# Channel attention followed by a gated convolution: decoding the filter taps earlier and moving the rounding copy of the gated product

## The chip, the cores and the metric

The kernel runs on one core of one Trainium2 chip. The metric is device time in microseconds (us) of one execution, from launch to the last write. Engines are named as in the profile: PE is TensorE (PEld its weight loads), DVE is VectorE, ACT is ScalarE, POOL is GpSimd, SP is SyncE, which here only issues transfers. A trailing q (SPq, ACTq) means the engine's instruction queue, where transfers are issued.

## The reference

```python
# q, k, v: (4, 6336, 256) float32; w_val, w_out: (256, 256); conv_w: (5, 256)
qn = q / (np.linalg.norm(q, axis=1, keepdims=True) + 1e-06)
kn = k / (np.linalg.norm(k, axis=1, keepdims=True) + 1e-06)
s = kn.transpose(0, 2, 1) @ qn / tau          # 256 x 256 scores per batch
a = softmax(s)                                 # over the last axis
x = v @ a                                      # (4, 6336, 256)
gate = sigmoid(sum over k of conv_w[k] * x shifted by k rows)   # 5 taps, causal
out = (gate * (x @ w_val)) @ w_out
```

The three small weight arrays arrive as 64-bit floating point numbers, everything else as float32. The attention is over channels: the scores of a batch are sums over its 6336 rows, so a batch's q and k have to be read to the end before its softmax, and only after that can its v be processed.

## The kernel before, in words

**Score groups.** The 6336 rows of q and k of a batch lie on 128 partitions with 49 rows each, and 64 rows remain. They are cut into 17 groups of three (the first and the fourth of two, the fourth with the remaining 64 rows). `load_group` (L78) issues the two transfers of a group on SP into one of six `raw` tiles, some groups ahead of use. `score_group` (L239) does three things with a group. It splits rows into a rounded part and a remainder (tile `hi`: an ACT cast at L269, a POOL subtraction at L270), for products in three fast passes. It squares the rows (L288, ACT, tile `sq`, three buffers) and adds the squares up for the norms (L293, on DVE for `acc_ps`, on POOL for `acc`). And it returns the matrix products (L316, PE, tile `s_ps`). In the first four groups of batches 0 and 1 no row is split, and the products are taken straight from `raw` in plain float32; in the other groups of batch 0 only the third row of a group, now and then none, is split.

**Weights.** As PE, ACT and POOL have no use for 64-bit numbers, DVE puts each weight together from its two words with integer operations: `decode` (L146 to L166) with ten operations for the taps (tiles `wk`, `wk_raw`, 10 partitions by 128, L204 and L206 the last two), `decode_past` for `w_val` (tiles `bits` and `wa`), and `decode` again for `w_out` (tile `wb`).

**Softmax.** `softmax` (L328) is a generator; each `tick()` emits one further stage at high priority. It makes `a`, its split form `w`, then turns `a` on PE (L395, into `at_ps`, one of four PSUM banks with the tag "bank"), copies it to `at` on ACT (L399) and multiplies it by `w_val` (L404), so that x @ w_val is one product of v as well.

**Steps.** The output is made in 13 chunks of 508 rows for each batch (52 steps). For a step, `transpose_v` (L436) turns v on PE (`t_ps`, tag "bank") and splits it on ACT and DVE; `conv` (L462) makes x in PSUM (`x_ps`, two buffers), takes the first tap on ACT (L469) and the other four on DVE (L471); `sigmoid` (L474) follows on ACT; `value` (L479) multiplies with x @ w_val; `split_g` (L491) rounds the product to `g_hi` on ACT (L502) and makes the remainder `g_lo` on POOL (L503); `finish` (L506) multiplies with w_out (`o_ps`, tag "bank"), copies the result to `o_sb` on ACT (L529) and stores it. In the main loop (L691) the steps of a batch run beside the score groups of the next batches, and beside its softmax.

**Order.** The order on each engine is made when the kernel is built, by a planner with simulated clocks: among the operations that it takes to be ready it issues the one that stands earliest in the program, with `high_priority` blocks ahead. Two things bind it: what an operation reads and writes, and `behind(...)` (L548), which puts an edge from a marked instruction to every later one of the same engine that is emitted within the block. It makes one engine's instruction stand behind another in its queue, and makes no engine wait for another. Tiles in one PSUM bank are given to one engine at a time.

Of the kernel before, what the change touches and what calls it, by code (L numbers as in the profile page):

```python
# [17 lines left out]
P = 128  # L18
# [6 lines left out]
EARLY = 2  # L25
# [6 lines left out]
def kernel(  # L32
# [45 lines left out]
    def load_group(b, g):  # L78
        j0, n = groups[g]
        t = raw_p.tile([P, 2, GROUP, C], F32, name="raw")  # L80
        for s, src in ((0, q), (1, k)):
            main = src[b, 0:RP * P].rearrange("(p j) c -> p j c", j=RP)
            last_load[0] = nc.sync.dma_start(out=t[:, s, 0:n, :], in_=main[:, j0:j0 + n, :])  # L83
            if rest_of(g):
                nc.sync.dma_start(out=t[0:REST, s, n, :], in_=src[b, RP * P:N])
        raws[b, g] = t

    for g in range(3):
# [150 lines left out]
    def score_group(b, g):  # L239


        n = groups[g][1]
        raw = raws.pop((b, g))
        rows_of = raw.rearrange("p s j c -> p j s c")
        if b == 0:
            if g < FIRST_SPLIT:
                nw, nv = GROUP, 2
            else:
                nw, nv = GROUP - 1, 2 + (g % 4 == 3)
        else:  # L250
            nw, nv = (GROUP, 2 * (g % 2 == 0)) if b == 1 and g < LEAD else (0, 2)
        parts = [(P, 0, n)]
        if rest_of(g):
            parts.append((REST, n, 1))
        if g == 0:
            state[b] = dict(
                s=ps_s.tile([P, NH, C], F32, name="s_ps"),
                acc=ps_s.tile([P, 2, C], F32, name="acc_ps"),
                side=acc_p.tile([P, 2, C], F32, name="acc"),
                begun=set(),  # L260
            )
        st = state[b]
        split = [(np_, max(j0, nw), j0 + nj) for np_, j0, nj in parts if j0 + nj > nw]
        hi = split_p.tile([P, GROUP, 2, 2, C], F32R, name="hi") if split else None
        sq = split_p.tile([P, GROUP, 2, C], F32, name="sq")
        cast = None
        for np_, ja, jb in split:
            r, js = slice(0, np_), slice(ja, jb)
            cast = nc.scalar.copy(hi[r, js, :, 0, :], rows_of[r, js])  # L269
            nc.gpsimd.tensor_tensor(hi[r, js, :, 1, :], rows_of[r, js], hi[r, js, :, 0, :].bitcast(F32), ALU.subtract)  # L270
        rows = [(np_, j) for np_, j0, nj in parts for j in range(j0, j0 + nj)]

        def norms():

            where = {}
            squares = [(np_, j0, j0 + nj) for np_, j0, nj in parts]
            for key in ("acc", "side"):
                if key not in st["begun"]:

                    full = [j for np_, j in rows if np_ == P and (j < nv) == (key == "acc")]  # L280
                    if full:
                        st["begun"].add(key)
                        where[full[0]] = key
                        nc.scalar.activation(st[key], rows_of[:, full[0]], AF.Square)
                        squares = [(np_, x, y) for np_, ja, jb in squares
                                   for x, y in ((ja, min(jb, full[0])), (max(ja, full[0] + 1), jb)) if x < y]
            for np_, ja, jb in squares:
                nc.scalar.activation(sq[0:np_, ja:jb], rows_of[0:np_, ja:jb], AF.Square)  # L288
            for np_, j in rows:
                if j in where:  # L290
                    continue
                eng, key = (nc.vector, "acc") if j < nv or np_ < P else (nc.gpsimd, "side")
                add = eng.tensor_tensor(st[key][0:np_], st[key][0:np_], sq[0:np_, j], ALU.add)  # L293
                if eng is nc.vector:
                    marks["ADD"] = add

        late = b == 1 and 0 < g < LEAD
        with tc.issue_after(cast.ins) if cast else nullcontext():
            if owed:
                owed.pop()()  # L300
            if b == 1 and LEAD <= g < LEAD + OWE:
                owed.append(norms)
            elif not late:
                norms()

        def mms(np_, j):
            r = slice(0, np_)
            stop = g == NG - 1 and np_ == parts[-1][0] and j == parts[-1][1] + parts[-1][2] - 1
            for h in range(NH):
                hs = slice(h * P, (h + 1) * P)  # L310
                if j < nw:
                    ops = [(raw[r, 1, j, hs], raw[r, 0, j, :])]
                else:
                    ops = [(hi[r, j, 1, x, hs], hi[r, j, 0, y, :]) for x, y in ((0, 0), (0, 1), (1, 0))]
                for n_, (lhs, rhs) in enumerate(ops):
                    marks["SCORES"] = nc.tensor.matmul(st["s"][:, h, :], lhs, rhs, start=False,  # L316
                                                       stop=stop and h == NH - 1 and n_ == len(ops) - 1)

        def clear():

            nc.tensor.matmul(st["s"].rearrange("p h c -> p (h c)"), zeros[:, 0:P], zeros, start=True, stop=False)

        if late:
            later.append(norms)
        return ([clear] if g == 0 else []) + [lambda np_=np_, j=j: mms(np_, j) for np_, j0, nj in parts for j in range(j0, j0 + nj)]


    def softmax(b):  # L328
# [63 lines left out]
        at_ps = ps.tile([P, 512], F32, name="o_ps", tag="bank")  # L392
        for h in range(NH):
            for h2 in range(NH):
                nc.tensor.transpose(at_ps[:, (h2 * NH + h) * P:(h2 * NH + h + 1) * P],  # L395
                                    a[:, h, h2 * P:(h2 + 1) * P], ident)
        yield
        at = soft_p.tile([P, NH, C], F32, name="at")
        note("ACT", nc.scalar.copy(at.rearrange("p h c -> p (h c)"), at_ps))  # L399
        yield  # L400
        aw_ps = ps.tile([P, 512], F32, name="o_ps", tag="bank")
        for h in range(NH):
# [59 lines left out]
    def conv(b, i, h):  # L462
        w = chunks[i][1]
        if h == 0:
            gates[b, i] = w_p.tile([P, NH, WMAX], F32, name="gate")
        gate = gates[b, i]
        x_ps = ps.tile([P, 512], F32, name="x_ps", bufs=2)
        product(x_ps[:, 0:HALO + w], weights[b], 0, b, i, h, 0, HALO + w)
        marks["TAP"] = nc.scalar.activation(gate[:, h, 0:w], x_ps[:, 0:w], AF.Copy, scale=cw[:, h:h + 1])  # L469
        for tap in range(1, K):  # L470
            marks["GATE"] = nc.vector.scalar_tensor_tensor(gate[:, h, 0:w], x_ps[:, tap:tap + w], cw[:, tap * NH + h:tap * NH + h + 1],  # L471
                                                           gate[:, h, 0:w], ALU.mult, ALU.add)
# [33 lines left out]
    def finish(b, i):  # L506
# [4 lines left out]
        o_sb = w_p.tile([P, NT, C], F32, name="o_sb")  # L511
        for j in range(0, nt, 2):
            pair = offs[j:j + 2]
            o_ps = ps.tile([P, 512], F32, name="o_ps", tag="bank")
            for u, off in enumerate(pair):
                n_ = 0
                for h in range(NH):
                    for gs, ws in ((gh, wo_hi), (gh, wo_lo), (gl, wo_hi)):
                        nc.tensor.matmul(o_ps[:, u * C:(u + 1) * C], gs[:, h, off:off + P], ws[:, h, :],  # L519
# [2 lines left out]
            if (b, i) == all_steps[-1]:  # L522

                for u, (copy, dma) in enumerate(((nc.scalar.copy, nc.scalar), (nc.vector.tensor_copy, nc.sync))[:len(pair)]):
                    copy(o_sb[:, j + u, :], o_ps[:, u * C:(u + 1) * C])
                    first = max((j + u) * P - pair[u], 0)
                    dma.dma_start(out=out[b, t0 + pair[u] + first:t0 + pair[u] + P], in_=o_sb[first:P, j + u, :])
                continue
# [60 lines left out]


    for n in range(NG):
        if n == 1:
            load_taps()
            load_weights(0)
            for _ in prepare_weights(2):
                pass
            prep.append(prepare_weights(0))
        if n == NG - 4:
            load_upto(NG + 1)
# [5 lines left out]
                load_v(*step(1))  # L605
        with behind(*(["SPIN"] if n < 2 else [])):
            run_group()
        if n == 0:
            with behind("SCORES"):
                spin(4)  # L610
        if n == 9:
            with behind("SCORES", "ADD"):
                spread_tau()
# [41 lines left out]
    tick()  # L655
    for h in range(NH):
        conv(*step(0), h)
    marks["TAP0"] = marks["TAP"]
    while stages:
        tick()  # L660
    for h in range(NH):
# [29 lines left out]
    for n in range(len(all_steps)):  # L691
# [1 line left out]
        if step(n + VLEAD + 1):  # L693
            load_v(*step(n + VLEAD + 1))
        turns = due_after(n) - (issued - len(ready))
        if n == 0:
            sigmoid(*now)
        for turn in range(turns):
            if turn == 0:
                run_group()  # L700
                with behind(*(["ACT", "VH", "SIG"] if n < EARLY else ["ACT"])):
                    split_group()
        tick()
        if n:
# [12 lines left out]
        with end(n + 1):  # L717
            value(*now)
        tick()
        with end(n + 1):  # L720
            split_g(*now)
        for turn in range(turns):
            if turn == 1:
                run_group()
                with behind(*(["TAP", "GH"] if n < EARLY else ["ACT"])):
                    split_group()
        if new:
            for h in range(NH):
                transpose_v(*new, h)
        tick()  # L730
        if prev:
            with behind(*{len(all_steps) - 2: ["CONV"], len(all_steps) - 1: ["G"]}.get(n, [])):
                finish(*prev)
# [33 lines left out]
```

## Time and profile before

| what | value |
|---|---|
| runs of the kernel before | 649.90, 649.97 and 649.16 us; median 649.9 |
| profiled execution, its own time | 649.27 us |
| span of the profile, first to last instruction | 647.4 us |
| PE busy | 635.9 us, 98% of the span |
| DVE, ACT, POOL busy | 523.4, 470.9 and 391.3 us |
| mean granted TensorE clock | 0.995 of full speed |

Times inside the span start at the span's first instruction. In a row of the timeline the first number is the start, the second the time taken, then come engine, line, operation, what is written from what, shape and count; a bracket at the end gives the idle time of the engine before the row and what ended it. In the view of waits a row has the total in us, the count and the longest.

### The profile page before, as it was taken

Reading aid. Unit: us, or ns where it says so; the run is one execution under the profiler, and the core shown is the slowest. Engines: PE = TensorE matmul, PEld = TensorE weight load, DVE = VectorE, ACT = ScalarE, POOL = GpSimd, SP = SyncE. Lnnn points to the kernel's source line nnn. Section 1 sums busy time; section 2 is a strip of 40 time slices with the busy share of each in tenths; the row PEclk is TensorE's granted clock in tenths of the full one; section 3 lists DMA queues with packets and bytes.
Section 4 is the critical chain, followed back from the end, with each engine's and each line's share of the span. In section 5 each row is a group of like instructions: output and inputs, shape, how many; then the busy total and the mean of one; then the engine's idle time right before and its main releaser. Section 6 shows DMA issues by size and latency. Waiting matters only on the chain.

```text
span 647.4 us, 10814 instructions
## 1 busy us (share of the span) xinstructions
PE 635.9 (98%) x4051; PEld 573.0 (89%) x4051; DVE 523.4 (81%) x826; ACT 470.9 (73%) x620; POOL 391.3 (60%) x205
## 2 busy tenths in 40 slices
PE   9999999999999999999999999999999999999996
PEld 7888889999888999999998989999998898888886
DVE  4999798787787878878787869777878889888884
ACT  5677797858787697778788688778679565655564
POOL 2784599768655598859765559686775222212221
PEclk9989999999999999999999999999999999999998
DMA  8989665455434556545543546552322343343213
GB/s 299 402 294 347 207 230 172 151 191 184 128 118 146 196 177 207 181 147 174 166 159 99 190 154 223 189 170 66 97 80 67 123 132 110 106 131 107 64 41 111
DMA packets 73674, 105.77 MB, mean 163 GB/s; under 512 B 4300, under 2 KB 55702, under 8 KB 73622
## 3 DMA queue, kind: packets, MB, share of 16 engines
q1 hardware_dynamic: 47846, 79.76, 37.0%
q10 hardware_dynamic: 25776, 25.32, 12.5%
q8 instruction: 32, 0.52, 0.3%
q14 instruction: 20, 0.16, 0.1%
HBM read 79.11 MB, written 25.95 MB: 162 GB/s over the span
## 4 chain that ended last, share of the span: by engine, by line
PE 86%; DVE 5%; ACT 3%; POOL 2%; issue 1%; DMA 1%; SPq 1%; ACTq 0%; POOLq 0%
PE o_ps L519 21%; PE x_ps L455 20%; PE s_ps L316 19%; PE val_ps L455 19%; PE t_ps L445 6%; DVE gate L471 2%; DMA raw<-in_k_dram 1%; POOL hi L270 1%; PE o_ps L404 1%; DVE acc_ps L293 1%; SPq L83 0%; ACT L477 0%; ACT L375 0%; ACT sq L288 0%; POOL g_lo L503 0%
## 5 line engine op out<-in xcount | busy, mean ns | idle before, releaser
L471 DVE SCALAR_TENSOR_TENSOR gate<-x_ps,cw,gate 128x508 f32<-128x508 f32 (+1 forms) x416 | 276.6, 720 | 12.6 <-ACT gate L469 10.6
L270 POOL TENSOR_TENSOR hi<-raw,hi 128x1536 fp32r<-128x1536 f32 (+3 forms) x62 | 180.3, 2911 | 81.7 <-ACT hi L269 81.7
L503 POOL TENSOR_TENSOR g_lo<-gate,g_hi 128x1016 fp32r<-128x1016 f32 (+1 forms) x50 | 116.2, 2324 | 110.2 <-ACT g_hi L502 101.1
L293 DVE TENSOR_TENSOR acc_ps<-acc_ps,sq 128x512 f32<-128x512 f32 (+1 forms) x135 | 94.1, 697 | 71.0 <-ACT sq L288 68.6
L455 PE MATMUL x_ps<-v_hi,w 128*128 128x512 f32 (+1 forms) x416 | 140.2, 394 | 0.9 <-DVE rz L379 0.9
L316 PE MATMUL s_ps<-hi 128*128 128x256 f32 (+1 forms) x912 | 131.6, 289 | 2.8 <-POOL hi L270 2.6
L455 PE MATMUL val_ps<-v_hi,w 128*128 128x508 f32 (+1 forms) x416 | 133.8, 383 | 0.0
L316 PEld LDWEIGHTS s_ps<-hi 128*128 128x128 f32 (+1 forms) x912 | 118.6, 191 | 7.7 <-POOL hi L270 3.6
L529 ACT COPY o_sb<-o_ps 128x512 f32<-128x512 f32 x99 | 58.2, 588 | 78.3 <-PE o_ps L519 78.1
L519 PE MATMUL o_ps<-wo_hi,g_hi 128*128 128x256 f32 x400 | 113.3, 283 | 1.3 <-ACT at L399 1.3
L519 PE MATMUL o_ps<-wo_hi,g_lo 128*128 128x256 f32 x400 | 112.3, 281 | 0.0
L519 PE MATMUL o_ps<-wo_lo,g_hi 128*128 128x256 f32 x400 | 112.2, 281 | 0.0
L288 ACT ACTIVATE sq<-raw 128x1536 f32<-128x1536 f32 (+2 forms) x72 | 96.0, 1342 | 4.9 <-DVE acc_ps L293 3.9
L455 PEld LDWEIGHTS x_ps<-v_hi,w 128*128 128x128 f32 x416 | 77.4, 188 | 15.3 <-ACT z L377 1.3
L455 PEld LDWEIGHTS val_ps<-v_hi,w 128*128 128x128 f32 x416 | 77.1, 188 | 13.6
L293 POOL TENSOR_TENSOR acc<-acc,sq 128x512 f32<-128x512 f32 x57 | 74.5, 1306 | 23.2 <-ACT sq L288 23.0
L469 ACT ACTIVATE gate<-x_ps,cw 128x508 f32<-128x508 f32 (+1 forms) x104 | 68.4, 670 | 20.8 <-PE x_ps L455 20.2
L269 ACT CAST hi<-raw 128x1536 fp32r<-128x1536 f32 (+3 forms) x62 | 76.8, 1241 | 5.7 <-PE s_ps L316 2.0
L446 ACT CAST v_hi<-t_ps 128x512 fp32r<-128x512 f32 (+1 forms) x104 | 56.1, 567 | 33.9 <-PE t_ps L445 31.3
L455 PE MATMUL x_ps<-v_lo,w 128*128 128x512 f32 (+1 forms) x208 | 79.6, 382 | 0.0
L455 PE MATMUL val_ps<-v_lo,w 128*128 128x508 f32 (+1 forms) x208 | 79.1, 380 | 0.0
L489 DVE TENSOR_TENSOR gate<-val_ps,gate 128x508 f32<-128x508 f32 (+1 forms) x104 | 64.1, 658 | 17.4 <-ACT gate L477 17.2
(114 smaller groups left out, 819.4 us busy)
## 6 DMA issues: line engine op xcount, KB each, us to landing
raw<-in_q_dram SPq DMA_DIRECT2D x60, 384.0 KB
raw<-in_k_dram SPq DMA_DIRECT2D x60, 384.0 KB
v_raw<-in_v_dram SPq DMA_DIRECT2D x44, 512.0 KB
out_dram<-o_sb ACTq DMA_DIRECT2D x47, 384.0 KB
out_dram<-o_sb ACTq DMA_DIRECT2D x47, 124.0 KB
raw<-in_q_dram SPq DMA_DIRECT2D x8, 256.0 KB
raw<-in_k_dram SPq DMA_DIRECT2D x8, 256.0 KB
v_raw<-in_v_dram SPq DMA_DIRECT2D x4, 384.0 KB
```

What stands on the lines that cost most here:

```text
L269: cast = nc.scalar.copy(hi[r, js, :, 0, :], rows_of[r, js])
L270: nc.gpsimd.tensor_tensor(hi[r, js, :, 1, :], rows_of[r, js], hi[r, js, :, 0, :].bitcast(F32), ALU.subtract)
L288: nc.scalar.activation(sq[0:np_, ja:jb], rows_of[0:np_, ja:jb], AF.Square)
L293: add = eng.tensor_tensor(st[key][0:np_], st[key][0:np_], sq[0:np_, j], ALU.add)
L316: marks["SCORES"] = nc.tensor.matmul(st["s"][:, h, :], lhs, rhs, start=False, stop=stop and h == NH - 1 and n_ == len(ops) - 1)
L455: marks["PRODUCT"] = nc.tensor.matmul(ps, wt[:, which, ws, ch, hs], vs[:, ch, lo:hi_], start=ws == 0 and ch == 0 and vs is th, stop=ws == ...
L469: marks["TAP"] = nc.scalar.activation(gate[:, h, 0:w], x_ps[:, 0:w], AF.Copy, scale=cw[:, h:h + 1])
L471: marks["GATE"] = nc.vector.scalar_tensor_tensor(gate[:, h, 0:w], x_ps[:, tap:tap + w], cw[:, tap * NH + h:tap * NH + h + 1], gate[:, h, 0 ...
L489: nc.vector.tensor_tensor(gate[:, h, 0:w], vals[h][:, 0:w], gate[:, h, 0:w], ALU.mult)
L503: nc.gpsimd.tensor_tensor(gl[:, :, 0:w], gate[:, :, 0:w], gh[:, :, 0:w].bitcast(F32), ALU.subtract)
L519: nc.tensor.matmul(o_ps[:, u * C:(u + 1) * C], gs[:, h, off:off + P], ws[:, h, :], start=n_ == 0, stop=n_ == 3 * NH - 1)
L529: marks["ACT"] = nc.scalar.copy(o_sb[:, j:j + len(pair), :], o_ps[:, 0:len(pair) * C].rearrange("p (j c) -> p j c", c=C))
```

## The change

Part by part:

1. The transfer of the second group of batch 0 is issued in two pieces for each of q and k: its first row of each partition, then the other two (`load_group`).
2. `load_taps()` and the ten decoding operations of the taps (`prepare_weights(2)`) come before the first group in the program, right behind the loads of groups 0 to 2, in place of before the second group. `load_weights(0)` stays where it was.
3. The four idle products on `warm` (`spin(4)`) behind the first group become two, behind the first row of the second group (`pause`).
4. At the first step, `sigmoid` is emitted behind the first score group, and the split of the next group isn't put behind it any more. The squares that a group owes (`owed`) go behind the last `sigmoid`. From the third step on, the first split of a step goes behind the last `g_hi` as well as behind the last copy of results.
5. `split_g` goes behind the first tap of the last convolution. In a step with stages of a softmax still to come it is also emitted later, after the turning of v and another stage, and behind the copy `at`. The turning of v goes behind the turning of `a`.
6. In the last step the two halves of the last pair have a PSUM bank each.

```diff
     def load_group(b, g):
...
+        for ja, jb in ((0, 1), (1, n)) if (b, g) == (0, 1) else ((0, n),):
+            for s, src in ((0, q), (1, k)):
...
+                last_load[0] = nc.sync.dma_start(out=t[:, s, ja:jb, :], in_=main[:, j0 + ja:j0 + jb, :])
...
             if owed:
-                owed.pop()()
+                with behind("SIG"):
+                    owed.pop()()
...
+        def pause():
+            with behind("SCORES"):
+                spin(2)
+
+        products = ([clear] if g == 0 else []) + [...]
+        if (b, g) == (0, 1):
+            products.insert(1, pause)
...
-                nc.tensor.transpose(at_ps[:, (h2 * NH + h) * P:(h2 * NH + h + 1) * P],
+                marks["AT"] = nc.tensor.transpose(at_ps[:, (h2 * NH + h) * P:(h2 * NH + h + 1) * P],
...
+        at_copy = nc.scalar.copy(at.rearrange("p h c -> p (h c)"), at_ps)
+        marks["ATC"] = at_copy
...
         marks["TAP"] = nc.scalar.activation(gate[:, h, 0:w], x_ps[:, 0:w], AF.Copy, scale=cw[:, h:h + 1])
+        if h == 0:
+            marks["TAP0"] = marks["TAP"]
...
+            halves = [o_ps, ps.tile([P, 512], F32, name="o_ps", tag="bank") if last and len(pair) > 1 else o_ps]
...
-                    copy(o_sb[:, j + u, :], o_ps[:, u * C:(u + 1) * C])
+                    copy(o_sb[:, j + u, :], halves[u][:, u * C:(u + 1) * C])
...
     for n in range(NG):
-        if n == 1:
+        if n == 0:
             load_taps()
-            load_weights(0)
             for _ in prepare_weights(2):
                 pass
+        if n == 1:
+            load_weights(0)
             prep.append(prepare_weights(0))
...
-        if n == 0:
-            with behind("SCORES"):
-                spin(4)
...
-        if n == 0:
-            sigmoid(*now)
         for turn in range(turns):
             if turn == 0:
                 run_group()
-                with behind(*(["ACT", "VH", "SIG"] if n < EARLY else ["ACT"])):
+                if n == 0:
+                    sigmoid(*now)
+                with behind(*(["ACT", "VH"] + ["SIG"] * (n > 0) if n < EARLY else ["ACT", "GH"])):
                     split_group()
...
-        with end(n + 1):
-            split_g(*now)
+        turning = bool(stages)
+        if not turning:
+            with end(n + 1), behind("TAP0"):
+                split_g(*now)
...
         if new:
-            for h in range(NH):
-                transpose_v(*new, h)
+            with behind("AT"):
+                for h in range(NH):
+                    transpose_v(*new, h)
         tick()
+        if turning:
+            with behind("TAP0", "ATC"):
+                split_g(*now)
```

More of the change, by code (lines that the diff above doesn't have):

```diff
@@ L80, in load_group @@
         t = raw_p.tile([P, 2, GROUP, C], F32, name="raw")
[L81 to L85, printed above, removed]
+        for ja, jb in ((0, 1), (1, n)) if (b, g) == (0, 1) else ((0, n),):
+            for s, src in ((0, q), (1, k)):
+                main = src[b, 0:RP * P].rearrange("(p j) c -> p j c", j=RP)
+                last_load[0] = nc.sync.dma_start(out=t[:, s, ja:jb, :], in_=main[:, j0 + ja:j0 + jb, :])
+                if rest_of(g):
+                    nc.sync.dma_start(out=t[0:REST, s, n, :], in_=src[b, RP * P:N])
         raws[b, g] = t
@@ L324, in score_group @@
             later.append(norms)
-        return ([clear] if g == 0 else []) + [lambda np_=np_, j=j: mms(np_, j) for np_, j0, nj in parts for j in range(j0, j0 + nj)]
+        def pause():
+            with behind("SCORES"):
+                spin(2)
+        products = ([clear] if g == 0 else []) + [lambda np_=np_, j=j: mms(np_, j) for np_, j0, nj in parts for j in range(j0, j0 + nj)]
+        if (b, g) == (0, 1):
+            products.insert(1, pause)
+        return products
     def softmax(b):
@@ L394, in softmax @@
             for h2 in range(NH):
-                nc.tensor.transpose(at_ps[:, (h2 * NH + h) * P:(h2 * NH + h + 1) * P],
-                                    a[:, h, h2 * P:(h2 + 1) * P], ident)
+                marks["AT"] = nc.tensor.transpose(at_ps[:, (h2 * NH + h) * P:(h2 * NH + h + 1) * P],
+                                                  a[:, h, h2 * P:(h2 + 1) * P], ident)
         yield
         at = soft_p.tile([P, NH, C], F32, name="at")
-        note("ACT", nc.scalar.copy(at.rearrange("p h c -> p (h c)"), at_ps))
+        at_copy = nc.scalar.copy(at.rearrange("p h c -> p (h c)"), at_ps)
+        note("ACT", at_copy)
+        marks["ATC"] = at_copy
         yield
@@ L513, in finish @@
             pair = offs[j:j + 2]
+            last = (b, i) == all_steps[-1]
             o_ps = ps.tile([P, 512], F32, name="o_ps", tag="bank")
+            halves = [o_ps, ps.tile([P, 512], F32, name="o_ps", tag="bank") if last and len(pair) > 1 else o_ps]
             for u, off in enumerate(pair):
                 n_ = 0
+                o_ps = halves[u]
                 for h in range(NH):
@@ L657 @@
         conv(*step(0), h)
-    marks["TAP0"] = marks["TAP"]
     while stages:
```

## The prediction

> **What bounds the kernel.** I read the head of the page first, then the waits of PE. The page gives the share, the waits give the places.
>
> ```profile
> span 647.4 us, 10814 instructions
> PE 635.9 (98%) x4051; PEld 573.0 (89%) x4051; DVE 523.4 (81%) x826; ACT 470.9 (73%) x620; POOL 391.3 (60%) x205
> ```
> ```profile
> PE s_ps L316 <- POOL hi L270: 2.6, 2, 1.4
> PE o_ps L519 <- ACT at L399: 1.3, 2, 1.0
> ```
>
> PE is idle for 647.4 - 635.9 = 11.5 us of the whole span, start and end included. The change adds and removes next to no product, so it can only win inside these 11.5 us and where products ran slowly, and what PE wins anywhere is kept, as PE is full afterwards. So I went from wait to wait of PE in the timeline and asked of each whether an edit reaches it.
>
> **The wait at 30 us, and the taps' decoding (edit 2).** The rows below are, in this order, of POOL, DVE, ACT and PE from 11 to 39 us; the last two are sums by windows, of all engines and of DVE at the taps' tile alone.
>
> ```profile
> 11.61 1.27 POOL L293 TENSOR_TENSOR acc<-acc,sq 128x512 f32<-128x512 f32 x1 [10.11 <-ACT sq L288]
> ...
> 18.19 1.29 POOL L270 TENSOR_TENSOR hi<-raw,hi 128x512 fp32r<-128x512 f32 x1 [0.51 <-ACT hi L269]
> ...
> 29.20 1.27 POOL L293 TENSOR_TENSOR acc<-acc,sq 128x512 f32<-128x512 f32 x1 [3.21 <-ACT sq L288]
> ```
> ```profile
> 18.29 1.27 DVE L158 TENSOR_SCALAR wk<-wk 10x128 int32<-10x128 int32 x1
> ...
> 20.68 0.33 DVE L160 TENSOR_SCALAR wk<-wk 10x128 int32<-10x128 int32 x1
> ...
> 24.88 1.25 DVE L204 SCALAR_TENSOR_TENSOR wk<-wk_raw,wk 10x128 f32<-10x128 int32 x1
> ```
> ```profile
> 27.57 1.49 ACT L288 ACTIVATE sq<-raw 128x1536 f32<-128x1536 f32 x1 [3.20 <-DVE acc_ps L293]
> ```
> ```profile
> 25.05 1.06 PE L316 MATMUL s_ps<-hi 128*128 128x256 f32 x6
> ...
> 27.49 1.06 PE L316 MATMUL s_ps<-hi 128*128 128x256 f32 x6
> ...
> 31.76 0.85 PE L316 MATMUL s_ps<-hi 128*128 128x256 f32 x5 [1.37 <-POOL hi L270]
> 32.54 0.38 PE L233 MATMUL tau_ps<-tau_sb,ones 1*128 1x1 f32 x2
> 32.85 3.64 PE L316 MATMUL s_ps<-raw 128*128 128x256 f32 x8
> 35.92 1.31 PE L316 MATMUL s_ps<-hi 128*128 128x256 f32 x6
> 38.61 1.06 PE L316 MATMUL s_ps<-hi 128*128 128x256 f32 x6
> ```
> ```profile
> 33.00:37.00 4.00, 4.00 (x14) 3.29 (x15) 3.93 (x7) 2.58 (x3) 3.65 (x3) 0.57 0.74 288
> 14.00:27.00 13.00, 7.83 (x9) 1.00 1.03 401
> ```
>
> Followed backwards: PE waits 1.37 us for a subtraction on POOL, which stands behind an addition that waited 3.21 us for squares, which waited 3.20 us for DVE to free a square buffer. DVE was at the taps: nine of the ten operations took 7.83 us (second windows row: DVE's busy time and count, of the taps' tile alone). They are on 10 partitions by 128 numbers. L158 took 1.27 us and its like L160 0.33; the long one started 0.10 us after a POOL subtraction of 1.29 us and ended with it, so I read the surplus as waiting for POOL. At 0.3 us each the ten take 3 us.
>
> The price on PE: the split products come every 27.49 - 25.05 = 2.44 us. From 27.49 to 38.61 three groups pass, which at that pace is 7.32 us; it took 11.12, so 3.80 too much. Of it 32.85 - 32.54 = 0.31 is the two small tau products, which stay. That leaves 3.5 us: 1.37 us of idling plus its start-up, and then half speed, as eight plain products took 3.64 us at a mean granted clock of 0.57 in this stretch. After the change the taps' transfer is SP's ninth issue in place of its thirteenth, POOL has its first addition at 11.61, and the decoding falls where POOL is mostly idle. I take the whole 3.5 us. The bounds: nothing if DVE is still late, 3.5 at most. Next behind it on that path is POOL itself, whose two 1.27 us operations a group fill 2.54 of the 2.44 us in groups that have both; from 37 us on the same mix holds the pace, so it costs at most a tenth here and there.
>
> By the Trainium skill (TensorE: Matmul & The Clock Gate, "Why this matters for your kernels") PE must idle for more than some 3 us before its clock drops, and a 1.37 us wait would not do it; then the slow window has another cause and stays, which by the rows below would leave 5.2 us of the sum. The trace has it after a 1.37 us wait. That is a rival below.
>
> **The start (edits 1 and 3).** PE, then ACT, then SP's first issue:
>
> ```profile
> 6.82 1.05 PE L103 MATMUL warm<-ones 128*128 128x128 f32 x8
> 7.96 10.13 PE L316 MATMUL s_ps<-raw 128*128 128x256 f32 x44
> ```
> ```profile
> 7.91 0.63 ACT L284 ACTIVATE acc<-raw 128x512 f32<-128x512 f32 x1 [2.46 <-DMA raw<-in_k_dram]
> ...
> 10.04 1.49 ACT L288 ACTIVATE sq<-raw 128x1536 f32<-128x1536 f32 x1 [0.56 <-DMA raw<-in_k_dram]
> ```
> ```profile
> 0.73 0.40 SPq L83 DMA_DIRECT2D raw<-in_q_dram  x1
> ```
>
> PE spends 6.82 to 7.87 on idle products and starts the second group when it lands at 7.91. With its first row landed earlier, 4 of its 12 products (10.13 / 44 = 0.23 us each) run before, 0.92 us; but the third group lands only at 10.04, and PE came to it at 7.96 + 12 x 0.23 = 10.7, so at most 0.6 can be won. Against it stand two more issues of a piece and the two of the taps ahead of the fourth group's loads. One takes SP 0.40 us, four 1.6, of which PE's 0.6 in hand at the third group and some of the fourth's are cover, so I bound the loss by 0.5 us. I take 0.2 won, as the bytes are the same and the transfers, not the issues, set the landings here.
>
> **The wait at 86 us (edit 4).** ACT, POOL and PE:
>
> ```profile
> 74.68 1.05 ACT L477 ACTIVATE gate<-gate 128x1016 f32<-128x1016 f32 x1 [1.12 <-DVE gate L471]
> 75.64 1.47 ACT L269 CAST hi<-raw 128x1536 fp32r<-128x1536 f32 x1
> ```
> ```profile
> 77.19 3.53 POOL L270 TENSOR_TENSOR hi<-raw,hi 128x1536 fp32r<-128x1536 f32 x1 [2.31 <-ACT hi L269]
> ...
> 84.27 3.53 POOL L270 TENSOR_TENSOR hi<-raw,hi 128x1536 fp32r<-128x1536 f32 x1
> ```
> ```profile
> 87.84 2.29 PE L316 MATMUL s_ps<-hi 128*128 128x256 f32 x17 [1.20 <-POOL hi L270]
> ```
>
> The cast stands behind the sigmoid, and POOL idles 2.31 us for it; from 77.19 on POOL works back to back until PE waits 1.20 us for it. With the cast free to go into ACT's 1.12 us of waiting ahead of the sigmoid, POOL starts up to 2.31 us earlier. The sigmoid is then later by at most 1.47 - 1.12 = 0.35 us, and the owed squares behind it, which POOL's additions need, take the cast's old place; nothing on PE waits for these. I take 1.0 of the 1.20 (bounds 0 and 1.2), since `g_lo` stands in between on POOL and can be no earlier than `g_hi`. The other new edge of this edit, casts behind `g_hi`, costs nothing: the copy of results, behind which they stood already, comes later than `g_hi` in its step.
>
> **The softmax waits (edit 5).** The first fence is of batch 2's softmax, the second of batch 3's.
>
> ```profile
> 345.09 1.05 ACT L502 CAST g_hi<-gate 128x1016 fp32r<-128x1016 f32 x1 [0.32 <-DVE gate L489]
> 347.08 0.60 ACT L399 COPY at<-o_ps 128x512 f32<-128x512 f32 x1
> 347.73 0.39 PE L519 MATMUL o_ps<-wo_hi,g_hi 128*128 128x256 f32 x1 [1.00 <-ACT at L399]
> ```
> ```profile
> 489.72 1.04 ACT L502 CAST g_hi<-gate 128x1016 fp32r<-128x1016 f32 x1 [0.44 <-DVE gate L489]
> 491.38 2.05 DVE L471 SCALAR_TENSOR_TENSOR gate<-x_ps,cw,gate 128x508 f32<-128x508 f32 x3 [0.56 <-ACT gate L469]
> 496.79 0.47 PE L455 MATMUL x_ps<-v_hi,w 128*128 128x512 f32 x1 [0.89 <-DVE rz L379]
> ```
>
> PE needs the bank that the copy `at` frees, and the copy stands behind `g_hi`, for which ACT idled 0.32 and worked 1.05 us. With `g_hi` behind the copy these 1.37 us go, more than PE's 1.00, and with them the 0.3 that the waits (1.3 in two) hold for batch 1: 1.3 us. In batch 3, ACT idles 0.44 us for `g_hi` while the first tap is behind it; with the tap first, DVE loses its 0.56 us of idling and its taps, which hold the bank that PE waits for, end that much earlier: 0.6 us. Together 1.9 (bounds 0 and 1.3 + 0.9 = 2.2). `g_hi` itself gets later by 1 to 2 us, `g_lo` behind it on POOL too; the results that need them are a step later, some 12 us.
>
> In ordinary steps `g_hi` behind the first tap costs ACT some waiting, where it came first before. The cover is ACT's idle time:
>
> ```profile
> 276.00:288.00 12.00, 12.00 (x82) 10.98 (x81) 9.57 (x16) 8.00 (x11) 7.15 (x3) 1.00 0.43 132
> ```
>
> In this step ACT (fourth engine, after PE, PEld and DVE) is busy for 8.00 of 12 us, so a microsecond of waiting is hidden; were it not, it would cost up to 1 us a step. I take nothing.
>
> **The end (edit 6).** ACT, DVE and SP:
>
> ```profile
> 642.09 0.37 ACT L525 COPY o_sb<-o_ps 128x256 f32<-128x256 f32 x1 [0.82 <-PE o_ps L519]
> 642.49 0.42 DVE L525 COPY o_sb<-o_ps 128x256 f32<-128x256 f32 x1 [2.27 <-ACT o_sb L525]
> 642.95 0.33 SPq L527 DMA_DIRECT2D out_dram<-o_sb  x1
> ```
>
> DVE copies after ACT, and SP issues the last store after DVE. With a bank each, DVE starts when PE is done, at 642.09: 0.4 us won (bounds 0 and 0.4), as everything from there to the end only shifts.
>
> **Sum.** 3.5 + 0.2 + 1.0 + 1.9 + 0.4 = 7.0 us off the profiled execution's 649.27 gives 642.3. That execution lies at the lower end of the runs (649.16 to 649.97), whose median is 0.6 higher, so I say 642.5.
>
> **Rivals.** (a) The clock stays: the slow window isn't the idling's doing. The plain products then still take 3.64 us for what their pace of 0.23 makes 1.84, so 1.8 us of the gain is missing: 644.3. For it speaks that PE's wait of 1.20 at 87.84 had no slow products behind it (17 in 2.29 us); against it, that the slow products are the first plain ones after the longest wait. (b) The taps' decoding is still in POOL's way or DVE is late for another reason, and all 3.5 remain: 646.0. The nearness of starts speaks for POOL as cause, that DVE also decodes `w_val` there speaks for this rival. (c) The planner, whose order shifts with every edge, gives the softmax and the first steps new waits as long as the old: 1.0 + 1.9 gone, 645.4. (d) Slower: DVE is in order, and the taps now stand ahead of the first additions. If DVE sits until they land (about 10 us, where the third group lands) and the ten then take their old 9 us, the first addition comes near 19; ACT, whose fourth square needs the first buffer and could follow the third by 12 us, is 7 us late, its casts and POOL with it. PE takes the subtraction that POOL ends at 18.19 + 1.29 = 19.48 at 25.05 - 2 x 2.44 = 20.17, so it has 0.7 us in hand, idles about 6 us and runs slowly for 1.8 more. With the 3.3 of the other edits won and the 3.5 of the old wait gone, that is 649.27 + 7.8 - 6.8 = 650.3. It decides once PE's new wait at the start passes 7 us. Against it: POOL isn't working then, so the ten should take 3 us, not 9.
>
> **Chances.** Forecast 0.58 (own range 641.0 to 643.8), (a) 0.10, (b) 0.11, (c) 0.15, (d) 0.06. A measurement of this kernel can tell about 0.2%, 1.3 us, from no change. (a) to (c) stay faster than that unless two meet: faster 0.88, same 0.06, slower 0.06. The range holds the forecast with its bounds and (a) to (c), 640.6 to 646.6.
>
> **What will show it.** Right: taps' operations of 0.2 to 0.4 us before 16 us, split products every 2.44 us from 18 to 50 us, a granted clock of 1.00 there; PE's waits for POOL `hi` and ACT `at` gone from the list; the last two copies side by side. Wrong: a PE wait in the first 20 us, a slow window that moved, or new waits for ACT `g_hi` or `hi` in the steps, which would sum to what is missing.

## The result and the profile after

| kernel | median of its runs | lowest to highest | ratio to before, 95% interval |
|---|---|---|---|
| before | 649.47 us | 649.16 to 649.97 | |
| changed | 643.48 us | 642.80 to 644.07 | 0.9907 [0.9893, 0.9922] |

The change takes 6.0 us off by medians. The profiled execution of the changed kernel took 642.80 us with a span of 641.0, against 649.27 and 647.4: 6.4 us less span. The head of the page after, and PE's list of waits:

```profile
span 641.0 us, 10812 instructions
PE 632.9 (99%) x4047; PEld 571.4 (89%) x4047; DVE 518.9 (81%) x826; ACT 470.1 (73%) x620; POOL 391.3 (61%) x205
```
```profile
PE warm L104 <- DVE ones L96: 1.0, 1, 1.0
PE s_ps L318 <- DMA raw<-in_k_dram: 0.9, 1, 0.9
PE x_ps L466 <- DVE gate L484: 0.2, 1, 0.2
PE s_ps L318 <- ACT hi L270: 0.2, 1, 0.2
```

PE's idle time went from 11.5 to 8.1 us; its busy time fell by 3.0, of which 1.7 is the stretch at half clock that this profile doesn't have. The waits for POOL `hi` and for ACT `at` are gone. One is new: 0.9 us for the load of the third group. PE, from 8 us on:

```profile
8.03 1.89 PE L318 MATMUL s_ps<-raw 128*128 128x256 f32 x8
10.82 7.54 PE L318 MATMUL s_ps<-raw 128*128 128x256 f32 x32 [0.90 <-DMA raw<-in_k_dram]
18.01 1.07 PE L318 MATMUL s_ps<-hi 128*128 128x256 f32 x6
...
27.90 1.06 PE L318 MATMUL s_ps<-hi 128*128 128x256 f32 x6
28.80 1.89 PE L318 MATMUL s_ps<-raw 128*128 128x256 f32 x8
30.34 1.06 PE L318 MATMUL s_ps<-hi 128*128 128x256 f32 x6
31.33 0.38 PE L234 MATMUL tau_ps<-tau_sb,ones 1*128 1x1 f32 x2
31.64 1.99 PE L318 MATMUL s_ps<-raw 128*128 128x256 f32 x8
...
47.92 1.06 PE L318 MATMUL s_ps<-hi 128*128 128x256 f32 x6
...
49.61 1.07 PE L456 MATMUL t_ps<-ident,v_raw 128*128 128x128 f32 x8
```

The eight plain products at 31.64 take 1.99 us where they took 3.64. Two operations of the taps' decoding (DVE), and the POOL operation beside the second:

```profile
12.26 0.22 DVE L159 TENSOR_SCALAR wk<-wk 10x128 int32<-10x128 int32 x1
...
15.74 1.31 DVE L167 TENSOR_TENSOR wk_raw<-wk_raw,wk 10x128 int32<-10x128 int32 x1
```
```profile
15.64 1.27 POOL L271 TENSOR_TENSOR hi<-raw,hi 128x512 fp32r<-128x512 f32 x1 [2.04 <-ACT hi L270]
```

The line that took 1.27 us in the prediction's rows (L158 there, L159 here) takes 0.22 where POOL was idle when it began (POOL's next operation starts at 12.34); the one that starts 0.10 us behind a POOL operation takes 1.31 and ends 0.14 behind it.

Where the time came from shows by taking the start of the same product in both traces and subtracting (after less before): +0.3 us at 12 us, -2.9 at 37, -3.2 at 83, -4.7 at 90, -6.6 at the end of the last product; from there to the end of the span it is 5.54 us where it was 5.35. These figures are of one profile each; where the text below compares the starts of the same products, the measure is again the first profile of the kernel before.

### The profile page after: what moved, and what is told of

Read it like the earlier page. It is cut to its first block, busy times and chain, and to the rows that moved or that the text cites. A ratio compares the mean times of both kernels' runs of the same rounds, so it can differ in the third digit from the quotient of the medians.

```text
span 641.0 us, 10812 instructions
## 1 busy us (share of the span) xinstructions
PE 632.9 (99%) x4047; PEld 571.4 (89%) x4047; DVE 518.9 (81%) x826; ACT 470.1 (73%) x620; POOL 391.3 (61%) x205
## 4 chain that ended last, share of the span: by engine, by line
PE 92%; ACT 3%; DVE 1%; DMA 1%; issue 1%; SPq 0%; ACTq 0%
PE s_ps L318 23%; PE o_ps L535 21%; PE x_ps L466 20%; PE val_ps L466 20%; PE t_ps L456 6%; PE o_ps L415 1%; DMA raw<-in_k_dram 1%; DVE gate L484 1%; SPq L84 0%; ACT L490 0%; ACT gate L490 0%; ACT g_hi L515 0%; ACT hi L270 0%; ACT v_hi L457 0%; ACT s L384 0%
## 5 line engine op out<-in xcount | busy, mean ns | idle before, releaser
L502 DVE TENSOR_TENSOR gate<-val_ps,gate 128x508 f32<-128x508 f32 (+1 forms) x104 | 64.1, 657 | 17.5 <-ACT gate L490 17.4
```

The source lines that it names most:

```text
L502: nc.vector.tensor_tensor(gate[:, h, 0:w], vals[h][:, 0:w], gate[:, h, 0:w], ALU.mult)
```

## The experiments

Each run stands beside runs of the kernel before on the same chip, whose medians were 649.46 to 649.90 us. A result is given as its median, the lowest and highest run, and the ratio to the kernel before with its 95% interval.

**The taps by themselves.** The kernel before with edit 2 alone, and the kernel before with the taps decoded where they always were, but through a scratch tile in PSUM in place of SBUF:

```diff
-        if n == 1:
+        if n == 0:                    # e1_taps: load_taps and prepare_weights(2) ahead
             load_taps()
-            load_weights(0)
             prepare_weights(2)
+        if n == 1:
+            load_weights(0)
```
```diff
-        yield from whole_words(w_raw["taps"], wk)          # e2_taps_psum
+        bank = ps.tile([P, 512], F32, name="tap_bits", tag="x_ps", bufs=2)
+        yield from whole_words(w_raw["taps"], wk, bank[0:K * NH, 0:P])
```

> The kernel before with edit 2 alone (taps loaded and decoded ahead of the first group; whole second group in one piece, four idle products). Theory: DVE, held up by POOL at the taps, makes the wait at 30 us, and the wait brings the slow window. Then the taps' operations take 0.2 to 0.4 us, PE's wait at 30 us and the slow window go, and the time is 649.5 - 3.4 = 646.1. Rival (DVE is late for other reasons): 649.5. Rival (the slow window has a cause of its own): wait gone, window there, 647.8. It also tells who made the third group land late in the changed kernel (ACT's square waited to 10.77 in place of 10.04): at 10.0 here it was the second group's two pieces, at 10.8 the taps' transfers.

> The kernel before, with the taps decoded at their old place but with PSUM as scratch (eleven operations in place of ten, none of which has both an input and the output, or two inputs, in SBUF alone). Theory: it is the sharing with POOL that held them up, not the place. Then they take 0.2 to 0.4 us each beside POOL, the wait at 30 us goes without any move, 646.1. Rival (the decoding is simply too early or too late there, whatever it costs): wait and window stay, 649.5.

e1_taps: 647.09 us (645.91 to 647.35), 0.9962 [0.9949, 0.9974]. e2_taps_psum: 646.30 (646.05 to 646.55), 0.9954 [0.9941, 0.9968]. So most of the 3.5 us at 30 us, 2.5 and 3.3 by medians, is bought by decoding faster, at either place. The first fence has operations of the kernel before in a second profile of it (b_again, below), the second the like ones with the scratch in PSUM, the third POOL's operation that runs beside the second:

```profile
21.55 1.27 DVE L162 SCALAR_TENSOR_TENSOR wk<-wk_raw,wk 10x128 int32<-10x128 int32 x1
22.85 1.20 DVE L164 TENSOR_SCALAR wk_raw<-wk_raw 10x128 int32<-10x128 int32 x1
24.08 1.26 DVE L166 TENSOR_TENSOR wk_raw<-wk_raw,wk 10x128 int32<-10x128 int32 x1
```
```profile
18.68 0.28 DVE L184 TENSOR_SCALAR tap_bits<-tap_bits 10x128 int32<-10x128 int32 x1
18.99 0.28 DVE L186 SCALAR_TENSOR_TENSOR tap_bits<-wk_raw,tap_bits 10x128 int32<-10x128 int32 x1
19.30 0.29 DVE L188 TENSOR_SCALAR tap_bits<-tap_bits 10x128 int32<-10x128 int32 x1
```
```profile
18.54 1.28 POOL L271 TENSOR_TENSOR hi<-raw,hi 128x512 fp32r<-128x512 f32 x1 [0.58 <-ACT hi L270]
```

Three DVE operations of 0.28 us end inside one POOL operation of 1.28; with all operands in SBUF each takes about as long as a POOL operation. The decoding isn't slow by its place, but by sharing SBUF with POOL. The Trainium skill (SBUF — State Buffer, "Who interferes with whom") calls the port pair that DVE and GpSimd share an exclusive lock: an operation of DVE with two SBUF inputs, or in a two-port mode, blocks for the whole of the other's. The rows agree, the SCALAR_TENSOR_TENSOR of 1.27 us against 0.28 above all. The TENSOR_SCALAR of 1.20 us has one SBUF input; that it ran in a two-port mode is what the rule would ask for, and no row shows it.

**Is it the clock or the lateness?** The prediction's sum puts about half of the 3.5 us down to slow products after the wait. Here PE's wait in front of that stretch is filled with idle products:

```diff
+        if (b, g) == (0, 9):          # e3_fill_wait, on the kernel before
+            def fill():
+                with behind("SCORES"):
+                    spin(5)
+            first = [lambda np_=np_, j=j: mms(np_, j) for np_, j0, nj in parts for j in range(j0, j0 + nj)]
+            return first[:-1] + [fill] + first[-1:]
```

> The kernel before with five idle products on PE (ten passes, about 1.1 us) just ahead of the split products that wait at 30 us. Nothing else is moved, DVE and POOL are as late as before. Theory: PE's idling brings the slow window. Then the window goes and the eight plain products after the wait take 1.9 in place of 3.64 us: 649.5 - 1.8 = 647.7. Rival (the window has another cause, since the wait is only 1.37 us long): it stays, 649.5.

650.36 us (648.83 to 651.01), 1.0011 [1.0002, 1.0020]: nothing won, 0.1% lost. PE's rows of it:

```profile
31.25 1.28 PE L103 MATMUL warm<-ones 128*128 128x128 f32 x10
32.29 1.31 PE L316 MATMUL s_ps<-hi 128*128 128x256 f32 x6
...
46.25 0.86 PE L316 MATMUL s_ps<-hi 128*128 128x256 f32 x5 [0.55 <-POOL hi L270]
53.56 0.70 PE L349 MATMUL o_ps<-acc_all,ones 128*128 128x256 f32 x2 [1.33 <-DVE acc_all L344]
```

The idle products end where the wait would have, nothing is slow behind them, and PE waits further on instead: 0.55 us for POOL, 1.33 for DVE's sum of squares. Whether filling the wait removed the slow stretch, or this execution wouldn't have had one, this run can't tell. That asked for a profile of the kernel before, unchanged, once more:

> The kernel before once more, for its profile: most of its runs have a mean clock of 0.998 to 1.000, so no slow window at 30 us, and yet take 649.2 to 650. Theory (DVE's lateness is the price, the window only one way of paying it): PE waits as before at 30 us and, where the products run at full speed after it, again between 40 and 54 us for POOL or DVE, about 3.4 us of lost time between 27 and 54 us in all. Rival (the window costs 1.8 by itself): without it the time is 647.7.

649.67 us (648.93 to 650.12), 1.0003 [0.9994, 1.0012]. Its profiled execution took 649.75 us with a granted clock of 1.00 throughout, so the slow stretch in the first profile is no fixed part of this kernel. Sums by windows (PE's busy time stands second, the granted clock after POOL's count): from 44 us on in the first profile of before, whose clock of 0.57 from 33 to 37 us the prediction shows; both windows in this one; and PE's waits in this one:

```profile
44.00:54.00 10.00, 10.00 (x63) 9.00 (x62) 9.04 (x17) 7.70 (x10) 6.20 (x5) 1.00 0.99 341
```
```profile
33.00:37.00 4.00, 4.00 (x23) 3.61 (x23) 3.93 (x8) 3.94 (x5) 4.00 (x4) 1.00 0.96 353
44.00:54.00 10.00, 8.93 (x54) 7.59 (x52) 9.08 (x16) 7.70 (x11) 6.33 (x5) 1.00 1.03 351
```
```profile
32.26 0.85 PE L316 MATMUL s_ps<-hi 128*128 128x256 f32 x5 [1.25 <-POOL hi L270]
...
45.69 0.86 PE L316 MATMUL s_ps<-hi 128*128 128x256 f32 x5 [0.47 <-POOL hi L270]
...
52.27 0.70 PE L342 MATMUL o_ps<-acc_all,ones 128*128 128x256 f32 x2 [0.60 <-DVE acc_all L337]
```

With the slow stretch there is no wait after it (10.00 of 10 us busy); without it PE, sooner there, waits 0.47 and 0.60 us more. From the first split product to the first turning of v it is 52.69 - 17.73 = 34.96 us with the slow stretch, 53.17 - 18.34 = 34.83 without, and 49.61 - 18.01 = 31.60 in the changed kernel. So the slow stretch adds next to nothing (0.13 us between the two). The other runs of the kernel before agree: of the 39 beside the experiments, the three with a mean clock of 0.995, as in the first profile, took 648.92, 649.35 and 649.58 us, and the 35 with 0.998 to 1.000 took 648.76 to 650.18 (one with 0.947 took 650.48). DVE is late, and PE pays 3.2 to 3.4 us for that in one form or the other.

**The taps in the changed kernel.** Edit 2 undone on the changed kernel, and the PSUM scratch in its place:

```diff
-        if n == 0:                    # e10_old_taps, on the changed kernel
+        if n == 1:
             load_taps()
+            load_weights(0)
             prepare_weights(2)
-        if n == 1:
-            load_weights(0)
```
```diff
 # e8_psum_after: the same, and e2's two lines in decode
 # e9_psum_start: e8_psum_after without edits 1 and 3 (the diff of e4_start below)
```

> The changed kernel without edit 2, taps decoded in SBUF at their old place. Theory: DVE is late again and the whole 3.4 us are back, 643.5 + 3.4 - 0.8 = 646.1, whether or not a window of half clock shows in the record. Rival (only the slow window cost time): 646.1 in runs that have it, 644.3 in those that do not.

> The changed kernel with edit 2 undone (taps loaded and decoded at the old place) and the taps decoded with PSUM as scratch. Theory: the taps' early transfers slow the loads behind them between 12 and 16 us (5.1 MB had landed by 18 us in place of 5.5) and so cost what the second group's pieces won; decoding beside POOL costs nothing with PSUM. Then the sixth group's cast is back near 17.5 us (18.4 to 18.5 in the changed kernel), and the time is 643.5 - 0.8 = 642.7, faster than both. Rival (the late landing is chance): 643.5, cast anywhere.

e10_old_taps: 646.58 us (645.53 to 647.16), 0.9956 [0.9943, 0.9968]. e8_psum_after: 642.38 (642.13 to 643.09), 0.9897 [0.9882, 0.9912]. e10's runs have a mean clock of 0.998 or 0.999, and its profile one of 1.00 throughout; so the rival by which only the slow stretch cost time, 644.3, falls. Edit 2 is worth 3.1 us in the changed kernel (646.58 against 643.48), and the scratch in PSUM 4.2 (646.58 against 642.38, intervals apart). By medians the version with PSUM beats both kernels, the changed one by 1.1 us; its interval overlaps the changed kernel's, as e2's does e1's (0.8 us there), so the sign is the same twice, but one comparison alone doesn't secure it.

The profiles show where such an advantage would come from. The fence has ACT's cast of the sixth group, the second one that is split, in e1_taps and then in e2_taps_psum:

```profile
19.55 0.62 ACT L269 CAST hi<-raw 128x512 fp32r<-128x512 f32 x1 [1.99 <-DMA raw<-in_k_dram]
```
```profile
17.84 0.62 ACT L270 CAST hi<-raw 128x512 fp32r<-128x512 f32 x1 [1.29 <-DMA raw<-in_k_dram]
```

It waits for the load. In the seven profiles with the taps' transfer early it starts at 18.4 to 19.7 us, in the seven with the transfer at its old place at 17.5 to 18.5. In five of the first seven PE itself waits for that load, 0.2 to 0.6 us; in none of the others. PE in the second profile of the changed kernel:

```profile
18.57 1.97 PE L318 MATMUL s_ps<-raw 128*128 128x256 f32 x8 [0.34 <-DMA raw<-in_k_dram]
```

So the early transfer, small as it is, goes along with a later load. By the starts of the same products PE falls behind by 0.1 to 1.3 us between 17.7 and 26 us in each of the first seven profiles, and by no more than 0.01 in any of the others. In e1_taps it is 0.8, as much as e1_taps lacks on e2_taps_psum. Edit 2 thus pays back a part of what it wins. SP's issues of the fifth group's k and of the taps, before and then after:

```profile
7.84 0.33 SPq L83 DMA_DIRECT2D raw<-in_k_dram  x1
8.81 0.35 SPq L143 DMA_DIRECT2D wk_raw<-in_moe_conv_w_dram  x1
```
```profile
4.50 0.41 SPq L144 DMA_DIRECT2D wk_raw<-in_moe_conv_w_dram  x1
...
10.70 0.33 SPq L84 DMA_DIRECT2D raw<-in_k_dram  x1
```

From about 6 us on SP waits for landings between its issues (0.2 to 1.4 us at a time in these two profiles). At their old place the taps' two transfers stood in that slow part of the queue; moved ahead, they leave it to the fifth group, whose k is issued at 9.86 to 10.91 us in the seven early profiles and at 7.84 to 8.97 in the other seven. That this delays the sixth group's landing fits, but no run separates it. The rate of all transfers between 12 and 16 us doesn't tell the two sorts apart: it was 309 GB/s in the profile after and 390 in that of before, but 307 and 318 also occurred with the transfer at its old place.

**The start (edits 1 and 3).** Undone on the changed kernel, and on e8_psum_after:

```diff
-        for ja, jb in ((0, 1), (1, n)) if (b, g) == (0, 1) else ((0, n),):   # e4_start
+        for ja, jb in ((0, n),):
...
-        if (b, g) == (0, 1):
-            products.insert(1, pause)
...
+        if n == 0:
+            with behind("SCORES"):
+                spin(4)
```

> The changed kernel without edits 1 and 3: second group in one piece, four idle products behind the first. Theory of the prediction: 0.2 slower than the changed kernel, 643.5. Rival (the pieces delay the third group): 0.3 to 0.9 faster, 642.7. Rival (the start makes no difference, POOL's first groups set the pace): the same.

> As the one before, and the start as in the kernel before (second group in one piece, four idle products). Theory: with the loads behind not slowed, the pieces now win their 0.5: this one is 0.3 to 0.6 slower, 643.1. Rival (POOL's and the loads' pace at the first groups take it back): the same as the one before.

> The changed kernel once more, as the measure for the three runs beside it: 643.1 to 643.5. It also tells whether the 0.9 us that PE waited for the third group's landing at 10.8 us belongs to the change: theory (the start of the transfers differs from run to run, as the second group began between 7.96 and 9.1 us in the kernels whose loads are unchanged): the wait is of another size here; rival (the two pieces or the taps' transfers delay the third group): 0.9 again.

e4_start: 643.07 us (642.54 to 643.65), 0.9896 [0.9882, 0.9909], beside the changed kernel once more (a_again): 643.70 (642.85 to 644.46), 0.9905 [0.9891, 0.9918]. e9_psum_start: 642.81 (642.52 to 643.28), 0.9901 [0.9887, 0.9914], beside e8's 642.38. Without the two edits it is 0.6 us faster in one pair and 0.4 slower in the other, all intervals overlapping. Inconclusive: whatever these edits are worth lies below what these runs tell apart. The landing they aim at varies by more: the third group's squares started at 9.93 to 11.23 us over the profiles of all kernels. ACT's row of it in the first and then in the second profile of the changed kernel:

```profile
10.77 1.48 ACT L289 ACTIVATE sq<-raw 128x1536 f32<-128x1536 f32 x1 [1.74 <-DMA raw<-in_k_dram]
```
```profile
9.93 1.49 ACT L289 ACTIVATE sq<-raw 128x1536 f32<-128x1536 f32 x1 [0.42 <-DMA raw<-in_k_dram]
```

PE doesn't wait for the third group in the second. So the wait of 0.90 us in the profile after belongs to that execution, not to the change, as the theory of a_again has it. At 12 us PE stands from 0.6 us ahead to 0.5 behind in the seven profiles with two pieces, and from level to 1.1 behind in the seven with one. That leans towards a gain from the pieces, but the ranges overlap and the times don't show it.

**The cast at 86 us (edit 4) and the softmax waits (edit 5).** Each undone on the changed kernel:

```diff
-                with behind("SIG"):                     # e5_cast
-                    owed.pop()()
+                owed.pop()()
...
+        if n == 0:                    # ahead of the score group again
+            sigmoid(*now)
...
-                if n == 0:
-                    sigmoid(*now)
-                with behind(*(["ACT", "VH"] + ["SIG"] * (n > 0) if n < EARLY else ["ACT", "GH"])):
+                with behind(*(["ACT", "VH", "SIG"] if n < EARLY else ["ACT"])):
```
```diff
-        turning = bool(stages)                          # e6_softmax
-        if not turning:
-            with end(n + 1), behind("TAP0"):
-                split_g(*now)
+        with end(n + 1):
+            split_g(*now)
...
-            with behind("AT"):
-                for h in range(NH):
-                    transpose_v(*new, h)
+            for h in range(NH):
+                transpose_v(*new, h)
...
-        if turning:
-            with behind("TAP0", "ATC"):
-                split_g(*now)
```

> The changed kernel without edit 4 (cast behind the first sigmoid again, owed squares free, casts not bound to g_hi). Theory: the wait of PE for POOL hi near 82 us is back with 1.2 us: 643.3 + 1.3 = 644.6. Rival (the earlier groups' new lead hides it): 643.3 and no such wait.

> The changed kernel without edit 5 (g_hi free, turning of v free). Theory: PE's waits for the copy at (0.3 and 1.0 us) and for DVE in batch 3 (0.9) are back, 643.3 + 1.9 = 645.2. Rival (other waits take their place in the changed kernel, so nothing was won): 643.3.

e5_cast: 645.57 us (644.36 to 645.69), 0.9931 [0.9918, 0.9943]; e6_softmax: 645.26 (644.69 to 646.34), 0.9933 [0.9919, 0.9947]; a_again beside both: 643.70. So edit 4 is worth 1.9 us by medians and edit 5 1.6; e5_cast's interval touches that of a_again, e6_softmax's lies just beyond it. PE's waits in e5_cast, then in e6_softmax:

```profile
PE s_ps L317 <- POOL hi L271: 1.2, 1, 1.2
```
```profile
PE o_ps L535 <- ACT at L408: 1.3, 2, 1.0
PE x_ps L466 <- DVE rz L388: 0.9, 1, 0.9
```

Each edit taken back brings its own waits back, with their old lengths. e5's profile also has a slow start (PE waits for the sixth group's load as above), so of its 1.9 us some is not edit 4's. The starts of the same products leave the start out: between 60 and 92 us PE gains 1.2 to 1.6 us in the eight profiles with edit 4 and 0.0 in e5_cast, and between 92 and 510 us 1.9 to 2.0 in the eight with edit 5 and 0.0 in e6_softmax.

**The end (edit 6).** The last pair in one bank again, on the changed kernel:

```diff
-            halves = [o_ps, ps.tile([P, 512], F32, name="o_ps", tag="bank") if last and len(pair) > 1 else o_ps]
+            halves = [o_ps, ps.tile([P, 512], F32, name="o_ps", tag="bank") if False else o_ps]
```

> The changed kernel without edit 6 (both halves of the last pair in one PSUM bank again). Theory: the copies go one after the other, SP issues the last store 0.4 us later, and the end is 0.4 later: 643.9, with 5.3 us or more from PE's last product to the end of the span. Rival (two stores issued side by side take longer to land, so that nothing was won): 643.5 and the same distance as in the changed kernel, 5.5 us.

643.11 us (643.03 to 643.33), 0.9905 [0.9892, 0.9919], against 643.48 with 0.9907: no gain from the edit. ACT's and DVE's last copies and SP's last issue, after and then without edit 6:

```profile
635.39 0.37 ACT L541 COPY o_sb<-o_ps 128x256 f32<-128x256 f32 x1 [0.72 <-PE o_ps L535]
...
635.51 0.42 DVE L541 COPY o_sb<-o_ps 128x256 f32<-128x256 f32 x1 [1.88 <-PE o_ps L535]
...
635.96 0.33 SPq L543 DMA_DIRECT2D out_dram<-o_sb  x1
```
```profile
635.82 0.37 ACT L541 COPY o_sb<-o_ps 128x256 f32<-128x256 f32 x1 [0.82 <-PE o_ps L535]
...
636.23 0.42 DVE L541 COPY o_sb<-o_ps 128x256 f32<-128x256 f32 x1 [2.28 <-ACT o_sb L541]
...
636.68 0.33 SPq L543 DMA_DIRECT2D out_dram<-o_sb  x1
```

The copies do run side by side, and SP issues 0.5 us after PE's last product (635.96 - 635.47) where it was 0.9 (642.95 - 642.05). But the last packet of SP's queue, which stands here for the store's landing, ends at 639.67, 3.7 us after the issue; before it ended at 646.24, 3.3 after. From the last product to it, it is 4.20 us against 4.19. Without edit 6 in the changed kernel it is 4.20 as well (639.98 - 635.78), with the issue 0.9 us after the last product. So the landing doesn't follow this issue; what sets it isn't shown.

## Why the prediction was right, and where not

The forecast of 642.5 us lies 1.0 below the median, and its five terms, 7.0 us in all, gave 6.0 by medians and 6.5 by the two profiled executions. The step from 642.3 to 642.5 is a guess: by the prediction's own reading (a median 0.6 above the profile) it should have been 642.9, and 642.5 fits only because the median over all five runs, 649.47, lies 0.2 above. Of the signs that it named, the clock, the pace of the split products, the vanished waits and the copies side by side came true. One did not: seven of the taps' ten operations took 0.2 to 0.3 us, but three took 0.69, 1.31 and 0.92, and the last began at 19.03 us, not before 16. And a PE wait in the first 20 us, named as a sign of being wrong, came with 0.90 us. Term by term:

- **The wait at 30 us, 3.5 predicted.** From +0.3 us at 12 us to -3.2 at 83 the trace gives 3.5; edit 2 undone gives 3.1, alone 2.5 (with PSUM 3.3). The size and the cause (DVE held up by POOL) hold. The working of the size does not: "1.37 us of idling plus its start-up, and then half speed" describes what happened in that one profile and isn't the price, which was the same without half speed. That the sum came out is luck in this part. The runs put in its place: 3.2 to 3.4 us of lateness of DVE, of which PE waits only what other losses haven't already taken. The right sum was to ask how late DVE is at the next point where PE needs it.
- **Rival (a), the slow clock stays.** It fell, and so did the question behind it: with the clock at 1.00 the kernel before took 649.75 us, with the slow stretch 649.27. By the rule of the Trainium skill that the prediction named (TensorE: Matmul & The Clock Gate, "Why this matters for your kernels"), a wait of 1.37 us doesn't lower the clock. The second profile of before, with full clock behind a wait of 1.25 us, agrees; the first, with the slow stretch behind 1.37, can't show whether the wait was its cause. Whether the idling has a part in it stays open.
- **The start, 0.2 predicted, not settled.** PE stood 0.3 us worse at 12 us in the first profile of the changed kernel (the third group landed at 10.77, and PE waited 0.90 for it) and 0.6 better in the second, so this term lies below what these profiles tell apart. The step that failed is "the bytes are the same and the transfers, not the issues, set the landings here": the loss was reckoned from 0.40 us of SP's time for each further issue, while the fifth group's k was issued up to 3 us later, behind SP's waits for landings, and the sixth group's load came later, for 0.1 to 1.3 us of PE. Rival (d), slower, named a PE wait at the start, but one of 6 us or more for DVE; DVE waited 1.2 us for the taps and then took 4.6 us for the ten operations, and PE's waits of 0.9 and 0.3 us are for loads.
- **The wait at 86 us, 1.0 predicted.** The trace gives 1.5 (-3.2 at 83 us to -4.7 at 90), e5_cast at most 1.9. The whole wait of 1.20 went: POOL `g_lo` in between didn't eat the 0.2 that was held back for it. The other 0.3, beyond the bound of 1.2, isn't traced to a row.
- **The softmax waits, 1.9 predicted.** -4.7 to -6.6, 1.9 by the trace; 1.6 by e6_softmax. New waits (rival c) are no more than 0.2 us. In ordinary steps the later `g_hi` costs PE nothing that the list shows.
- **The end, 0.4 predicted, nothing measured.** The step that failed is "everything from there to the end only shifts". The issue came 0.4 earlier, the landing behind it did not: an issue is no end, and of the term's bounds (0 and 0.4) the lower one came.

In the sum, what the trace shows is 3.5 + 1.5 + 1.9 won, 0.3 lost at the start and 0.2 at the end, behind the landing: 6.4 us, the difference of the spans.

## What to carry to other kernels

A late engine was paid for once here, and the wait was only the place where that showed: with the wait filled the payment moved on (e3_fill_wait), so look for what makes the engine late. The small operations of DVE that took as long as their neighbours on POOL were not slow but blocked; a PSUM tile as their scratch cured that where they stood, without moving a load. A transfer moved ahead changes places in the queue with those it passes, so look at what its old place held up. And an earlier issue of the last store counts only if the landing is earlier too.

## What the runs showed of the hardware

- The same integer operation on 10 partitions by 128 numbers took 1.27 us with its operands in SBUF beside a POOL operation, 0.28 with its output and one of its two inputs in PSUM beside a like one.
- A stretch of half clock of some 3.4 us (mean 0.57 over 33 to 37 us) appears in one profile of a kernel and not in the next, and the times don't tell which: 649.27 us with it, 649.75 without.
- Two stores issued 0.17 us apart (635.79 by ACT, 635.96 by SP): the last packet of the second one's queue ended 3.7 us after its issue; 0.46 us apart (642.49 and 642.95), 3.3. Both are 4.2 us after PE's last product.
